# S4 convolution and PEER experts on one core: remainders loaded once, two steps ordered later, more output buffers

## The chip, the cores and the metric

The kernel runs on 1 core of one Trainium2 chip. The metric is device time in microseconds (us), the median of the runs of a kernel. Before the change it is 1446.17 us, of 3 runs (1444.73, 1446.17, 1447.50). The core's engines are TensorE (PE, matmuls), VectorE (DVE), ScalarE (ACT), GpSimd (POOL) and SyncE (SP, which issues the DMAs).

## The reference

The input x is 2048 tokens of 576 channels. Branch `a` is an S4 convolution of the whole sequence; branch `b` is a mixture of 4096 one-neuron experts that are picked by product keys (32 heads, 64 keys per half, the best 2). A gate mixes the two for each token.

```python
def _A_ref(u, ...):
    P = exp(logdA[:, :, None] * l)                      # l = 0..2047
    K = einsum("dn,dnl,dn->dl", Cc, P, dB).real         # kernel, 576 x 2048
    y = irfft(rfft(pad(u)) * rfft(pad(K)))[:L]          # along the sequence
    return y + u * Dskip

def _B_ref(x, w_q, k1, k2, u, v):
    q = einsum("nd,dhc->nhc", x, w_q)                   # 32 heads x 256
    s1, s2 = q[..., :128] @ k1.T, q[..., 128:] @ k2.T   # 64 scores each
    ...                                                 # best 2 of each, best 2 of the 4 sums
    g = softmax(top_s)
    act = gelu(einsum("nd,nhkd->nhk", x, u[top_e]))
    return einsum("nhk,nhk,nhkd->nd", g, act, v[top_e])

g = sigmoid((x * gate_w).sum(-1))
return g * _A_ref(x, ...) + (1 - g) * _B_ref(x, ...)
```

## The kernel before

Nothing is gathered. The kernel computes all products of tokens and experts (`a` matmuls, x by u) and all scores (`s` matmuls, x by folded queries and keys), and then multiplies by weights that are zero where an expert wasn't picked. Every f32 operand is split in two f16 parts, high and low (`xb`, `uhl`, `whl`, `vhl`, `wh`), and a product is three matmuls: high by high, high by low, low by high. The channels are 576 = 4 x 128 + 64; the 64 left over are the remainder (`xr`, `ur`, `wrem`).

**The start.** `x_load` and `u_load` fetch the first 512 tokens of x and the first 512 experts of u: the remainder twice, into both halves of the partitions, and the four blocks of 128 channels in two DMAs (`halves_load`). `scale_first` squares them on ACT as they land (`sq`, into column sums `sc`), and PE adds the sums over the partitions; from that come the scales of the split. Between the two scales `x_norm(0)` runs eight filler matmuls on PE, whose result is overwritten.

**The main part.** `s` and `a` matmuls alternate by 512 columns. Beside them run, as generators: the splits of the next blocks of x, u and the queries; the generation of the convolution kernel K (`kb`); the first stage of a transform in two stages, for u (`u_stage1`: u is scaled and split into `uh`, the `u` matmuls follow, the result goes to `su_d` in DRAM) and for K (`k_stage1`: `k` matmuls into `k1o`, stored to `sk_d`); the products of both and the way back (`products`, with its `back`: `pv` matmuls into `vo`, stored to `z_d`); the selection of experts; and the scaled results of `a`, stored to `g_d`.

**The output stage.** For each of 16 token tiles PE builds the weights from one-hot codes (`S` matmuls of `A` and `Bg`, both made on DVE), DVE multiplies them with the results that were stored (`gl<-S,gl`), ACT and DVE split these (`wh`), and `o` matmuls multiply them by the experts' values. The values are scaled and split by `v_work` in eight chunks of 512 experts (`vhl`): the raw values of chunk c are loaded into the place of chunk c+1, the last into a place of its own (`vs`); the high part is made on ACT, the low part on DVE. `v_work` begins when `v_norm` has all squares of the values. `y` matmuls are the last stage of the transform (`y_part`); `ya` rows are the output.

**What sets the order.** The code is executed once, at build time, by a planner: generators wait in a heap, a clock runs on with every matmul, and an estimate of each engine's time says when a tile is ready. `ready(x, late=...)` holds a generator back until the planner takes x to be ready, plus `late` us. Each engine then runs its instructions strictly in the order in which the planner issued them, with semaphores for the true dependences; all loads and nearly all stores are on one queue, SP's. An edit of a `late` or of a number of buffers therefore moves everything that the planner decides later.

All instructions but a few are recorded in three helpers: L134 (an operation of ACT, DVE or POOL), L205 (a DMA), L214 (a matmul).

Of the kernel before, what the change touches and what calls it, by code (L numbers as in the profile page):

```python
# [24 lines left out]
D = 576  # L25
# [113 lines left out]
def body(ctx: ExitStack, tc: tile.TileContext, xT, au, par, logdt, dskip, gatew, wq, kT, uT, vv,  # L139
# [281 lines left out]
    idx = wj.tile([128, NT, 64, 2], F16, name="idx")  # L421
    xb = []

    def halves_load(a, src, c):

        columns.add(a.tensor.name)
        for m in (0, 2):
            dma(a[:, m:m + 2], src[128 * m:128 * m + 256, c].rearrange("(k p) n -> p k n", p=128))

    def x_load(tb):  # L430
        a = slot([4, 512], F32, f"xs{tb}")
        r = pl.tile([128, 512], F32, tag="xr", name=f"xr{tb}", bufs=2)
        c = slice(512 * tb, 512 * tb + 512)
        if tb > 0:
            dma(a, xT[0:512, c].rearrange("(k p) n -> p k n", p=128))
        dma(r[0:64], xT[512:576, c])
        dma(r[64:128], xT[512:576, c])
        if tb == 0:
            halves_load(a, xT, c)
        return a, r  # L440

    def squares(a, r, sq, dst):

        acc = newcol(), newcol()
        S.activation(sq[:, 0:4, :], a, AF.Square, accum_out=sc[:, acc[0]])
        S.activation(sq[:, 4, :], r, AF.Square, accum_out=sc[:, acc[1]])
        yield from ready(sq)
        tag = side()
        yield from need(tag)
        p = bank(tag, "sq")  # L450
        mm(p[:, 0:2], onesb, short(acc[0].start, 2), True, True, 0.05)
        yield from ready(p)
        V.tensor_reduce(out=dst, in_=p[:, 0:2], axis=AX, op=OP.add)
        free(tag, dst)
# [5 lines left out]
    def x_norm(tb, sq):  # L460

        yield from need("kb")
        p = bank("kb", f"x{tb}")
        if tb == 0:
            for k in range(8):
                mm(p, onesb, sq[:, k % 4, :], True, True)
            while not marks["s"]:
                yield 0.1
        for k in range(5):
            mm(p, onesb, sq[:, k, :], k == 0, k == 4)  # L470
        normed.append(tb)
# [27 lines left out]

    def scale_first(a, r, sq, keep=None):  # L500

        acc = [newcol() for _ in range(3)]
        yield from ready(r)
        S.activation(sq[:, 4], r, AF.Square, accum_out=sc[:, acc[0]])
        for n, m in enumerate((0, 2)):
            yield from ready(a[:, m:m + 2])
            S.activation(sq[:, m:m + 2], a[:, m:m + 2], AF.Square, accum_out=sc[:, acc[n + 1]])
        yield from ready(sq)
        yield from need("kb")
        p = bank("kb", "sq")  # L510
        for n in range(3):
            mm(p[:, 0:1], onesb, short(acc[n].start, 1), n == 0, n == 2, 0.05)
        yield from ready(p)
        out = root_scale(p[:, 0:1], 1.02)
        if keep is not None:
            V.tensor_copy(keep, p[:, 0:1])
        free("kb", out[0])
        return out
# [548 lines left out]
    def u_stage1():  # L1067
# [32 lines left out]
        for p in range(NT):  # L1100
# [7 lines left out]
            V.scalar_tensor_tensor(h[:, 1], a, s_u, h[:, 0], op0=OP.mult, op1=OP.subtract)  # L1108
            if p + 1 < NT:
                load(p + 1)  # L1110
            yield from ready(h)
            while ended[0] < p:
                yield 0.3
            tag = side()
# [23 lines left out]
    def k_stage1(ksb, fk, tabs):  # L1138
# [11 lines left out]
        for w in range(32):  # L1150
            tkt = tabs[w // 16]
            yield from ready(tkt, ksb)
            yield from enter()
            o = fk.tile([128, D], F32, tag="s1o", name=f"k1o{w}", bufs=4)
            pbs = []
            yield from need("wb", 2)
            for hh in range(2):
                pb = bank("wb", f"k1_{w}_{hh}")
                for n in range(2):
                    mm(pb[:, :288], tkt[:, w % 16, n], ksb[:, 2 * hh:2 * hh + 2, :, w, :].rearrange("p j c i -> p (j c) i"),  # L1160
                       n == 0, n == 1)
                pbs.append(pb)
            spawn(tail(w, o, pbs))
            del pb, pbs
# [3 lines left out]
    def products(ff):  # L1168
# [51 lines left out]
        def back(g, v):  # L1220
            for k, c, o, w in pieces(g):
                if k not in vos:
                    vos[k] = ff.tile([128, 2, D], F32, tag="vo", name=f"vo{k}", bufs=2)
            pvs = [bank("wb", f"pv_{g}_{n}") for n in range(2)]
            for n, (rows, cols) in enumerate(quads):
                mm(pvs[n // 2][cols, 0:PW], fi[rows, cols], v[rows, n % 2, :], True, True, 0.11)
            spawn(store(g, pvs))
# [85 lines left out]
    def u_load(c):  # L1313
# [6 lines left out]
        dma(r[64:128], uT[512:576, cs])  # L1320
        if c == 0:
            halves_load(a, uT, cs)
        return a, r

# [2 lines left out]
    def u_build(c):  # L1327
# [12 lines left out]
        if c == 0:  # L1340
            first_u[0] = hl
            s, i = yield from scale_first(a, r, sq, nu[:, 0:1])
            marks["s"].append(1)
        else:
            yield from squares(a, r, sq, nu[:, c:c + 1])
            s, i = root_scale(nu[:, c:c + 1], 1.02)
        if len(xb) == 4:
            V.tensor_scalar(i_a[:, c, :], i_x, i, None, op0=OP.mult)
# [510 lines left out]
```

## Time and profile before

| what | us |
|---|---|
| median of 3 runs | 1446.17 |
| the profiled execution, its time | 1444.99 |
| its span in the trace | 1443.2 |
| PE busy | 1422.5 |
| DVE busy | 1160.0 |
| ACT busy | 769.7 |
| POOL busy | 484.7 |
| first matmul of `a` starts at | 15.91 |
| first matmul of `S` starts at | 953.50 |
| first matmul of `o` starts at | 994.3 |

The span is 1.8 us shorter than the time of the same execution: what lies around it isn't in the trace. Times within the trace count from the start of the span. A row of the timeline reads: start, length, engine, line, operation, out<-in, shape, count; in brackets the time for which the engine stood idle before it, and what ended that. A row with a count of several is a run of such instructions, and its length reaches to the end of the last. Matmuls overlap, so the start of the next row says more than the length of one.

### The profile page before, as it was taken

How to read it: one execution, taken by the hardware profiler on the slowest of the kernel's cores; microseconds unless marked ns; L12 is line 12 of the kernel's file. 1: busy time of each engine (PE TensorE's matmuls, PEld its weight loads, DVE VectorE, ACT ScalarE, POOL GpSimd, SP SyncE). 2: the span in 40 equal slices, each digit the busy share in tenths (PEclk: the TensorE clock that was granted, in tenths of full speed). 3: DMA queues.
4: the chain of work that ended last, by engine and by line, in shares of the span. 5: the costliest groups of instructions: out<-in, count | busy, mean ns of one | idle time of the engine just before them, and what ended most of it. 6: DMA issues, size and time to landing. Idle time of an engine off the chain costs nothing.

```text
span 1443.2 us, 40781 instructions
## 1 busy us (share of the span) xinstructions
PE 1422.5 (99%) x16153; PEld 836.1 (58%) x16153; DVE 1160.0 (80%) x4590; ACT 769.7 (53%) x1277; POOL 484.7 (34%) x492
## 2 busy tenths in 40 slices
PE   7999999999999999999999999999999999999999
PEld 3444545455455445455555444456787787787785
DVE  6899899879886997875899897689877777867840
ACT  6346876786784876744655555666333224323310
POOL 0325347557266346230447899701000000000000
PEclk9999999999999999999999999999999999999999
DMA  9234323342334323159675677878433332442400
GB/s 309 74 114 154 105 74 120 124 145 72 108 100 154 93 87 120 49 173 310 210 259 196 241 257 275 274 234 262 156 124 127 126 122 86 142 149 69 159 10 18
DMA packets 134369, 215.70 MB, mean 149 GB/s; under 512 B 11041, under 2 KB 79905, under 8 KB 127777
## 3 DMA queue, kind: packets, MB, share of 16 engines
q1 hardware_dynamic: 134080, 213.06, 45.1%
q8 instruction: 127, 2.08, 0.6%
q14 instruction: 66, 0.53, 0.1%
q10 hardware_dynamic: 96, 0.02, 0.0%
HBM read 141.74 MB, written 71.30 MB: 148 GB/s over the span
## 4 chain that ended last, share of the span: by engine, by line
PE 86%; DVE 5%; DMA 1%; issue 0%; ACT 0%; SPq 0%; DVEq 0%; ACTq 0%
PE o L214 25%; PE s L214 24%; PE a L214 22%; PE S L214 3%; PE kb L214 2%; PE wb L214 2%; PE pr L214 2%; PE y L214 1%; PE kP L214 1%; PE pv L214 1%; PE u L214 1%; DVE vhl L134 1%; PE k L214 1%; DMA z_d<-vo 1%; DVE gl L134 1%; DVE A L134 1%
## 5 line engine op out<-in xcount | busy, mean ns | idle before, releaser
L214 PE MATMUL o<-vhl,wh 128*128 128x288 f16 (+2 forms) x3072 | 382.8, 286 | 0.0
L214 PE MATMUL s<-whl,xb 128*128 128x512 f16 x1536 | 363.9, 379 | 0.0
L214 PE MATMUL a<-xb,uhl 128*128 128x512 f16 x1536 | 358.9, 379 | 0.2 <-DVE go L134 0.2
L214 PEld LDWEIGHTS <-wh 128*128 128x128 f16 x3072 | 292.4, 98 | 84.1 <-issue 3.7
L214 PEld LDWEIGHTS <-xb 128*128 128x128 f16 x1792 | 170.7, 98 | 209.8 <-issue 15.2
L214 PEld LDWEIGHTS <-uhl 128*128 128x128 f16 x1536 | 147.7, 98 | 177.0 <-issue 3.5
L134 DVE FIND_INDEX8 i<-m,s 128x8 uint32<-128x64 f32 x1024 | 206.1, 219 | 0.0
L134 ACT ACTIVATE wh<-gl,s_wg 128x1024 f16<-128x1024 f32 x64 | 69.0, 1137 | 197.2 <-DVE gl L134 197.2
L134 DVE MAX8 m<-s 128x8 f32<-128x64 f32 x1024 | 145.8, 212 | 28.7 <-PE s L214 28.0
L134 POOL TENSOR_TENSOR CS<-CS,ex 128x512 f32<-128x512 f32 x72 | 98.0, 1392 | 147.5 <-DVE ex L134 146.1
L134 DVE TENSOR_TENSOR gl<-S,gl 128x256 f32<-128x256 f32 x256 | 88.4, 413 | 36.8 <-PE S L214 36.8
L134 ACT ACTIVATE go<-a,i_a 128x512 f32<-128x512 f32 x93 | 62.6, 685 | 94.5 <-PE a L214 68.4
L134 POOL TENSOR_TENSOR e<-aN,rt 128x512 f32<-128x512 f32 x72 | 83.3, 1178 | 49.9 <-PE kb L214 43.7
L134 DVE TENSOR_TENSOR A<-iota_a,vals 128x2048 f16<-128x2048 f16 x64 | 77.9, 1218 | 23.3 <-PE S L214 23.3
L134 ACT ACTIVATE gl<-gl 128x1024 f32<-128x1024 f32 x64 | 63.6, 1045 | 45.3 <-DMA gl<-g_d 45.3
L134 DVE SCALAR_TENSOR_TENSOR wh<-gl,s_wg,wh 128x1024 f16<-128x1024 f32 x62 | 77.6, 1279 | 12.4 <-ACT wh L134 12.3
L214 PE MATMUL s<-wrem,xb 128*128 128x512 f16 x256 | 76.2, 379 | 0.0
L214 PE MATMUL a<-xb,wrem 128*128 128x512 f16 x256 | 75.9, 379 | 0.0
L134 DVE MATCH_VALUE_LOAD i<-m,s 128x8 f32 x1024 | 69.4, 68 | 0.1
L134 ACT ACTIVATE CS<-CS 128x1024 f32<-128x1024 f32 x57 | 59.2, 1044 | 7.5 <-DVE CS L134 7.5
L134 POOL TENSOR_TENSOR ex<-ex,gN 128x512 f32<-128x512 f32 x36 | 44.8, 1255 | 53.2 <-ACT ex L134 53.0
L134 DVE SCALAR_TENSOR_TENSOR ya<-o,om,ya 128x288 f32<-128x288 f32 (+2 forms) x32 | 15.2, 513 | 54.9 <-PE o L214 54.9
(205 smaller groups left out, 2098.7 us busy)
## 6 DMA issues: line engine op xcount, KB each, us to landing
g_d<-go SPq DMA_DIRECT2D x128, 256.0 KB, 2.5
gl<-g_d SPq DMA_DIRECT2D x32, 1024.0 KB, 5.5
wq<-in_wq_dram SPq DMA_DIRECT2D x16, 1152.0 KB, 5.7
su_d<-us SPq DMA_DIRECT2D x32, 288.0 KB, 2.6
sk_d<-k1o SPq DMA_DIRECT2D x32, 288.0 KB, 2.9
ui<-su_d SPq DMA_DIRECT2D x16, 576.0 KB, 3.9
ki<-sk_d SPq DMA_DIRECT2D x16, 576.0 KB, 5.5
vn<-in_vv_dram SPq DMA_DIRECT2D x32, 288.0 KB, 5.4
```

The lines of the kernel that those rows point to most:

```text
L134: return f(*a, **k)
L214: T.matmul(o, l, r, start=start, stop=stop)
```

## The change

1. The first remainders of x and u are loaded once, into partitions 0 to 63; DVE copies them to 64 to 127. ACT squares 64 rows of them instead of 128, and memsets clear what isn't written. The four blocks of 128 channels come in three DMAs (two blocks, one, one) and are squared in three pieces, so four column sums are added on PE instead of three, for x and for u. Six fillers are left of eight.
2. The matmul on the squares of the second block of experts waits for the planner's estimate plus 2.0 us.
3. The `u` matmuls of the first two position transforms wait for the estimate of `uh` plus 1.8 us.
4. `k1o` has six buffers instead of four, `vo` three instead of two.

```diff
+    PARTS = ((0, 2), (2, 1), (3, 1))
     def halves_load(a, src, c):
         columns.add(a.tensor.name)
-        for m in (0, 2):
-            dma(a[:, m:m + 2], src[128 * m:128 * m + 256, c].rearrange("(k p) n -> p k n", p=128))
+        for m, n in PARTS:
+            dma(a[:, m:m + n], src[128 * m:128 * m + 128 * n, c].rearrange("(k p) n -> p k n", p=128))
...
         dma(r[0:64], xT[512:576, c])
-        dma(r[64:128], xT[512:576, c])
-        if tb == 0:
+        if tb > 0:
+            dma(r[64:128], xT[512:576, c])
+        else:
             halves_load(a, xT, c)
...
-    def squares(a, r, sq, dst):
+    def squares(a, r, sq, dst, late=0.0):
...
-        yield from ready(sq)
+        yield from ready(sq, late=late)
...
         if tb == 0:
-            for k in range(8):
+            for k in range(6):
                 mm(p, onesb, sq[:, k % 4, :], True, True)
...
     def scale_first(a, r, sq, keep=None):
-        acc = [newcol() for _ in range(3)]
+        acc = [newcol() for _ in range(1 + len(PARTS))]
+        if keep is None:
+            V.memset(sq[64:128, 4], 0.0)
+        V.memset(sc[64:128, acc[0]], 0.0)
         yield from ready(r)
-        S.activation(sq[:, 4], r, AF.Square, accum_out=sc[:, acc[0]])
-        for n, m in enumerate((0, 2)):
-            yield from ready(a[:, m:m + 2])
-            S.activation(sq[:, m:m + 2], a[:, m:m + 2], AF.Square, accum_out=sc[:, acc[n + 1]])
+        S.activation(sq[0:64, 4], r[0:64], AF.Square, accum_out=sc[0:64, acc[0]])
+        V.tensor_copy(r[64:128], r[0:64])
+        for n, (m, w) in enumerate(PARTS):
+            yield from ready(a[:, m:m + w])
+            S.activation(sq[:, m:m + w], a[:, m:m + w], AF.Square, accum_out=sc[:, acc[n + 1]])
...
-        for n in range(3):
-            mm(p[:, 0:1], onesb, short(acc[n].start, 1), n == 0, n == 2, 0.05)
+        for n, c in enumerate(acc):
+            mm(p[:, 0:1], onesb, short(c.start, 1), n == 0, n == len(PARTS), 0.05)
...
-            yield from ready(h)
+            yield from ready(h, late=1.8 if p < 2 else 0.0)
...
-            o = fk.tile([128, D], F32, tag="s1o", name=f"k1o{w}", bufs=4)
+            o = fk.tile([128, D], F32, tag="s1o", name=f"k1o{w}", bufs=6)
...
-                    vos[k] = ff.tile([128, 2, D], F32, tag="vo", name=f"vo{k}", bufs=2)
+                    vos[k] = ff.tile([128, 2, D], F32, tag="vo", name=f"vo{k}", bufs=3)
...
-            yield from squares(a, r, sq, nu[:, c:c + 1])
+            yield from squares(a, r, sq, nu[:, c:c + 1], 2.0 if c == 1 else 0.0)
```

(`u_load` changes as `x_load` does.) Three places of the order follow. On PE, where the square-sum of the second block of experts stands (`s_8` is the ninth group of scores; a row without "x" is one instruction), the order before has it behind three matmuls of that group:

```order
L214 MATMUL s_8_920<-whl_152,xb_519 128x512
L214 LDWEIGHTS xb_519
L214 MATMUL s_8_920<-whl_152,xb_519 128x512
L214 LDWEIGHTS xb_519
L214 MATMUL s_8_920<-whl_152,xb_519 128x512
L214 LDWEIGHTS onesb
L214 MATMUL sq<-sc,onesb 128x2
L214 LDWEIGHTS xb_519
L214 MATMUL s_8_920<-whl_152,xb_519 128x512
```

and the order of the change has it behind twelve, ahead of the two matmuls on the remainder:

```order
L214 MATMUL s_8_927<-whl_156,xb_526 128x512
L214 LDWEIGHTS xb_526
L214 MATMUL s_8_927<-whl_156,xb_526 128x512
L214 LDWEIGHTS onesb
L214 MATMUL sq<-sc,onesb 128x2
L214 LDWEIGHTS xb_526
L214 MATMUL s_8_927<-wrem_116,xb_526 128x512
L214 LDWEIGHTS xb_526
L214 MATMUL s_8_927<-wrem_116,xb_526 128x512
```

So it moved behind nine more matmuls. On PE again, where the second position transform (`u_1`) begins, before:

```order
L214 MATMUL s_14_1260<-whl_152,xb_598 128x512
L214 LDWEIGHTS xb_598
L214 MATMUL s_14_1260<-whl_152,xb_598 128x512
L214 LDWEIGHTS tu_1032
L214 MATMUL u_1_0_0_1286<-uh_1210,tu_1032 128x288
```

and with the change:

```order
L214 MATMUL s_14_1267<-wrem_116,xb_605 128x512
L214 LDWEIGHTS xb_605
L214 MATMUL s_14_1267<-wrem_116,xb_605 128x512
L214 LDWEIGHTS xb_605
L214 MATMUL s_15_1300<-whl_156,xb_605 128x512
L214 LDWEIGHTS xb_605
L214 MATMUL s_15_1300<-whl_156,xb_605 128x512
L214 LDWEIGHTS xb_605
L214 MATMUL s_15_1300<-whl_156,xb_605 128x512
L214 LDWEIGHTS tu_1006
L214 MATMUL u_1_0_0_1320<-uh_1217,tu_1006 128x288
```

Before it stood behind the ninth matmul of `s_14`; now it stands eight matmuls later, behind the third of `s_15`. The third place is on DVE, at the beginning of the output stage, where the last chunk of values (`vhl<-vs`) is split. Before, the first pair stands right ahead of these rows, and the second ends them, among the one-hot codes (`A`, `Be`, `Bg`) of the third tile, and its first `gl`:

```order
L134 TENSOR_TENSOR iwv<-sci 128x1
L134 TENSOR_SCALAR om<-gA 128x16
L134 TENSOR_SCALAR om<-om,iwv 128x16
L134 SCALAR_TENSOR_TENSOR wh_1_13596<-gl_0_13137,s_wg,wh_0_13595 128x1024
L134 TENSOR_TENSOR A_3_13854<-iota_a,vals 128x2048
L134 TENSOR_TENSOR Be_3_13856<-iota_b,vals 128x512
L134 TENSOR_TENSOR Bg_3_13858<-Be_3_13856,vals 128x512 x2
L134 TENSOR_TENSOR gl_0_13609<-S_0_0_13722,gl_0_13609 128x16x16
L134 TENSOR_TENSOR gl_1_13610<-S_0_0_13722,gl_1_13610 128x16x16
L134 TENSOR_TENSOR gl_0_13609<-S_0_1_13723,gl_0_13609 128x16x16
L134 TENSOR_TENSOR gl_1_13610<-S_0_1_13723,gl_1_13610 128x16x16
L134 SCALAR_TENSOR_TENSOR vhl_12500<-vs,sci,vhl_12500 128x576 x2
```

With the change they stand behind all sixteen `gl` of the third tile, among the rows of `ya` and two `wh`:

```order
L134 TENSOR_TENSOR ya_13645<-ya_13645,db 128x576
L134 TENSOR_TENSOR ya_13646<-ya_13646,db 128x576
L134 SCALAR_TENSOR_TENSOR vhl_12542<-vhl_12543,sci,vhl_12542 128x576 x2
L134 SCALAR_TENSOR_TENSOR ya_13645<-y_0_0_14120,iuk,ya_13645 128x288
L134 SCALAR_TENSOR_TENSOR ya_13645<-y_0_1_14125,iuk,ya_13645 128x288
L134 SCALAR_TENSOR_TENSOR wh_1_14088<-gl_0_13594,s_wg,wh_0_14087 128x1024
L134 SCALAR_TENSOR_TENSOR vhl_12543<-vs,sci,vhl_12543 128x576 x2
L134 SCALAR_TENSOR_TENSOR ya_13646<-y_1_0_14130,iuk,ya_13646 128x288
L134 SCALAR_TENSOR_TENSOR ya_13646<-y_1_1_14135,iuk,ya_13646 128x288
L134 SCALAR_TENSOR_TENSOR wh_1_14088<-gl_0_13594,s_wg,wh_0_14087 128x1024
L134 SCALAR_TENSOR_TENSOR vhl_12543<-vs,sci,vhl_12543 128x576 x2
```

What moved: from the `A` row that waits for the first `S` matmul to the last of these pairs, DVE has 9 sets of `A`, `Be` and two `Bg` in both orders; 36 `gl` before and 48 now; 10 pairs of `vhl` and 13; 5 `wh` and 9; and the six rows of `ya`, which stood behind. On PE, between the first `S` matmul and the second half of the eighth chunk of the first tile's `o`, there are 768 `S`, 180 `o` and 16 `y` in both, and 156 `a` before and 137 now. POOL makes one of the `wh` there instead of two.

More of the change, by code (lines that the diff above doesn't have):

```diff
@@ L1319, in u_load @@
         dma(r[0:64], uT[512:576, cs])
-        dma(r[64:128], uT[512:576, cs])
-        if c == 0:
+        if c:
+            dma(r[64:128], uT[512:576, cs])
+        else:
             halves_load(a, uT, cs)
```

## The prediction

> **What bounds the kernel now.** I read the page first, then the waits of TensorE (PE), then the timeline at each place that the change touches.
>
> ```profile
> span 1443.2 us, 40781 instructions
> PE 1422.5 (99%) x16153; PEld 836.1 (58%) x16153; DVE 1160.0 (80%) x4590; ACT 769.7 (53%) x1277; POOL 484.7 (34%) x492
> PEclk9999999999999999999999999999999999999999
> PE 86%; DVE 5%; DMA 1%; issue 0%; ACT 0%; SPq 0%; DVEq 0%; ACTq 0%
> ```
>
> PE is busy for 99% of the span at the full granted clock, and it is 86% of the chain that ended last. The change does not lessen its matmuls in any amount that counts: per source one more tiny square-sum and, once, two fewer fillers. So the time can move only where PE waits. The view of waits lists them, as engine, what waited, what it waited for, total us, times, longest:
>
> ```profile
> PE sq L214 <- ACT xb L134: 10.0, 3, 5.1
> PE sq L214 <- ACT uhl L134: 1.6, 1, 1.6
> PE k L214 <- ACT k1o L134: 1.4, 1, 1.4
> PE kb L214 <- issue: 1.4, 1, 1.4
> PE u L214 <- DVE uh L134: 1.4, 1, 1.4
> PE S L214 <- DVE gl L134: 0.7, 2, 0.5
> PE pv L214 <- ACT vo L134: 0.7, 1, 0.7
> ```
>
> Each edit has a row here: the remainders the first, the later squares the second, the later low words the fifth, six k1o buffers the third, three vo buffers the seventh. All but the first add up to 5.1 us. That is the size of the game: a third of a percent.
>
> **The change part by part.**
>
> *Remainders loaded once, blocks in three pieces.* The start, ScalarE (ACT) first:
>
> ```profile
> 4.35 0.63 ACT L134 ACTIVATE xb<-xr 128x512 bf16<-128x512 f32 x1 [2.12 <-DMA xr<-in_xT_dram]
> ...
> 6.96 1.06 ACT L134 ACTIVATE xb<-xs 128x1024 bf16<-128x1024 f32 x1 [1.89 <-DMA xs<-in_xT_dram]
> ...
> 9.09 1.06 ACT L134 ACTIVATE xb<-xs 128x1024 bf16<-128x1024 f32 x1 [0.98 <-DMA xs<-in_xT_dram]
> ...
> 11.21 1.06 ACT L134 ACTIVATE uhl<-us 128x1024 bf16<-128x1024 f32 x1 [0.36 <-DMA us<-in_uT_dram]
> ...
> 12.60 1.06 ACT L134 ACTIVATE uhl<-us 128x1024 bf16<-128x1024 f32 x1 [0.24 <-DMA us<-in_uT_dram]
> ```
>
> ```profile
> 10.31 3.57 PE L214 MATMUL x<-xb,onesb 128*128 128x512 bf16 x8
> 13.68 0.28 PE L214 MATMUL sq<-sc,onesb 128*128 128x1 bf16 x3
> 13.82 2.30 PE L214 MATMUL x<-xb,onesb 128*128 128x512 bf16 x5
> 15.91 0.52 PE L214 MATMUL a<-xb,uhl 128*128 128x512 f16 x1
> ```
>
> The squares follow the landings. Two halves of x, 512 KB each, landed 2.13 us apart (6.96, 9.09), so the 128 KB saved per source are worth 0.53 us: u's first half lands 0.5 to 1.1 us earlier, near 10.5. Behind it ACT needs 1.06 + 0.63 + 0.63 and the readout, and would be done near 13.0 instead of 13.7. I take 0.7 us (0.3 to 1.1; the number of transfers stays 8, so their issue costs nothing more). VectorE (DVE) copies the missing 64 rows while it waits for the first square-sum: nothing.
>
> The eight fillers run from 10.31 to 13.68, at 0.42 us each, up to u's square-sum without a hole. Six of them, from about 9.6, would end near 12.1, some 0.9 us ahead of that sum: a new hole in PE, a rival below.
>
> The Trainium skill, "TensorE: Matmul & The Clock Gate", under "What's actually happening", says that PE runs at half rate until a window of about 3.4 us was busy. The trace agrees with the slow start (0.42 us per 512 columns there, 0.22 later), though its clock row shows 9 from the first slice. By that rule a window that holds the hole would not count as busy, and the sum would be up to 1.7 us more (1451.3, an estimate from the rows above and this page); by the rows alone, where work broken by waits ran before 10.31 too, it stays as it is.
>
> *Squares and low words later.* One 512-column matmul takes 0.22 us (eight of s in 1.73 us):
>
> ```profile
> 79.71 1.89 PE L214 MATMUL s<-whl,xb 128*128 128x512 f16 x8
> 81.44 0.59 PE L214 MATMUL s<-wrem,xb 128*128 128x512 f16 x2
> ```
>
> The square-sum of the second expert block now stands nine matmuls later, 1.9 us, more than the 1.6 us that PE waited: gain 1.6 (bounds 0 and 1.6). The u matmuls of the second position transform stand eight later, 1.7 us. But their operand comes from DVE:
>
> ```profile
> 117.26 1.41 DVE L134 SCALAR_TENSOR_TENSOR uh<-us,sci,uh 128x576 f16<-128x576 f32 x1
> ...
> 60.00:126.00 66.00, 62.99 (x338) 28.88 (x337) 65.25 (x383) 24.98 (x46) 27.75 (x22) 1.00 0.34 105
> ```
>
> In this stretch (columns: length, then PE, PEld, DVE, ACT, POOL busy) DVE is busy for 65.25 of 66.0 us, so its uh moves only with the start. PE comes 1.6 earlier for the vanished hole and 1.7 later for the move: about 1.2 of the 1.4 us stay. Gain 0.2 (bounds 0 and 1.4).
>
> *Buffers.* k matmuls wait 1.4 us once for a k1o buffer whose store is late; two more buffers cover two more pairs of 0.4 us work and the s matmuls between them: gain 1.4 (bounds 0 and 1.4). The third vo buffer takes 0.7 (bounds 0 and 0.7). What is late next in both cases is PE itself.
>
> Gains: 0.7 + 1.6 + 0.2 + 1.4 + 0.7 = 4.6 us.
>
> *What the new order brings.* The planner replays everything after the two moved steps differently. Between 126 and 690 us PE was busy for 562.4 of 564, so a new wait there would cost as the rows above do, 1.4 to 1.6 us each; I take none (bounds 0 and 3, below nothing 1.4 if the kb row goes).
>
> One place can be worked out: where experts' values are split for the output stage. The first S matmuls release DVE here:
>
> ```profile
> 954.51 1.23 DVE L134 TENSOR_TENSOR A<-iota_a,vals 128x2048 f16<-128x2048 f16 x1 [1.32 <-PE S L214]
> ...
> 956.78 1.41 DVE L134 TENSOR_TENSOR gl<-S,gl 128x256 f32<-128x256 f32 x4
> 958.11 1.53 DVE L134 SCALAR_TENSOR_TENSOR vhl<-vhl,sci,vhl 128x576 f16<-128x576 f32 x2
> 959.56 1.41 DVE L134 TENSOR_TENSOR gl<-S,gl 128x256 f32<-128x256 f32 x4
> ...
> 963.43 2.74 DVE L134 TENSOR_TENSOR gl<-S,gl 128x256 f32<-128x256 f32 x8 [1.00 <-PE S L214]
> ...
> 968.20 1.27 DVE L134 SCALAR_TENSOR_TENSOR wh<-gl,s_wg,wh 128x1024 f16<-128x1024 f32 x1
> 969.40 1.54 DVE L134 SCALAR_TENSOR_TENSOR vhl<-vhl,sci,vhl 128x576 f16<-128x576 f32 x2
> ...
> 974.25 2.35 DVE L134 TENSOR_TENSOR Be<-iota_b,vals 128x512 f16<-128x512 f16 x1
> ...
> 1003.36 3.42 DVE L134 SCALAR_TENSOR_TENSOR vhl<-vs,sci,vhl 128x576 f16<-128x576 f32 x2
> ...
> 1011.90 1.54 DVE L134 SCALAR_TENSOR_TENSOR vhl<-vs,sci,vhl 128x576 f16<-128x576 f32 x2
> ```
>
> From the starts: a set A, Be, Bg takes 2.27 us, four gl 1.33, a pair of vhl 1.45, a wh 1.20. From the row at 954.51 to the last vhl pair the order before has 9 sets, 36 gl, 10 pairs, 5 wh and 1.0 us of small rows: 20.4 + 12.0 + 14.5 + 6.0 + 1.0 = 53.9 us. Measured are 58.9 (to 1013.4). The 5.0 between are the wait of 1.0 at 963.43 and two rows that were 1.9 longer than their like, at 974.25 and 1003.36; the second lies beside this one on GpSimd (POOL):
>
> ```profile
> 1002.89 2.54 POOL L134 TENSOR_TENSOR wh<-gl,wh 128x1024 f16<-128x1024 f32 x1 [26.56 <-ACT gl L134]
> 1017.21 1.42 DVE L134 TENSOR_TENSOR ya<-ya,db 128x576 f32<-128x576 f32 x2
> 1022.10 0.94 DVE L134 SCALAR_TENSOR_TENSOR ya<-y,iuk,ya 128x288 f32<-128x288 f32 x2
> 1019.53 6.67 PE L214 MATMUL o<-vhl,wh 128*128 128x288 f16 x53
> ```
>
> In the order of the change the same stretch has 9 sets, 48 gl, 13 pairs, 9 wh and the six ya: 20.4 + 16.0 + 18.9 + 10.8 + 3.2 + 0.3 = 69.6 us, 15.7 more. POOL has one such wh left instead of two: 1.9 less. So the last pair is done 13.8 us later after the first S than before.
>
> PE needs this pair in the second half of chunk 7 of the first o tile. Before, that is the 31st o matmul after 1019.53, at 0.126 us each: 1023.3, and the pair was done at 1013.4, 9.9 us of slack. In the new order PE has 19 fewer matmuls of a between the first S and that place (137 for 156): it comes 4.1 us sooner. 13.8 + 4.1 - 9.9 = **8.0 us of new wait**. Behind the waiting matmul the whole o stage is queued on PE, and nothing in it can be caught up. If the 1.0 and the last 1.9 also went, it would be 5.1; if both POOL rows' worth stayed, 9.9. I take 8.0, since the 53.9 and its three extras explain before to 0.1 us.
>
> Sum: 1444.99 (the profiled execution) - 4.6 + 8.0 = 1448.4. The median of the runs shown, 1446.17, is 1.2 above that execution, so **1449.6 us** on its scale.
>
> **The rivals.**
>
> *The extras fall away* (not slower). POOL's subtraction may lengthen nothing if it falls beside other DVE rows, and PE may not keep DVE waiting at the third S group. The wait is then 5.1, and 1446.17 - 4.6 + 5.1 = 1446.7. For it: POOL's row moves. Against: both rows beside POOL were lengthened before. It decides below 7.5 us of wait (4.6 + 2.9), from where the change is not slower by 0.2%.
>
> *The splits are not late* (faster): the buffers and moves do what they say, and DVE reaches the last pair before PE. 1446.17 - 4.6 = 1441.6. Against it stand the 15.7 us of added DVE rows in a stretch where DVE was already busy for 74.0 of 76 us:
>
> ```profile
> 954.00:1030.00 76.00, 75.27 (x1166) 48.44 (x1159) 74.02 (x131) 41.94 (x52) 4.77 (x2) 1.00 0.67 215
> ```
>
> *The hole behind six fillers keeps PE slow.* If PE stays at 0.42 us per matmul for another eight or so, it loses up to 1.7 us: 1451.3. For it: the first a matmul at full rate came only after 5.6 us of unbroken work. Against: the hole is under 1 us, and the work after it is unbroken. This is the rule of the page named above, as a case of its own.
>
> *A new wait in the reshuffled part*, two of 1.5: 1452.6. Nothing in the profile names its place.
>
> **How the numbers follow.** Forecast 0.42, extras gone 0.26, not late 0.20, slow PE 0.05, new waits 0.07. A measurement of this kernel can tell about 0.2%, 2.9 us: slower begins at 1449.1, faster ends at 1443.3. The forecast lies on that line, so I give it 0.30 slower and 0.12 within; with the two last rivals slower is 0.42. Within: 0.12 + 0.26 = 0.38. Faster 0.20. The range has to reach into the faster case and up to a wait of 9.9 with one new wait (1446.17 - 4.6 + 9.9 + 1.5 = 1453.0): 1442 to 1453. The slower half's own range is 1447.5 to 1453.
>
> **What would show it.** The row of sq on uhl gone; u on uh still near 1.2; k on k1o and pv on vo gone. The first a near 15.2 instead of 15.91, with a hole ahead of u's square-sum. Above all a new row, o waiting for DVE vhl, of some 8 us in all at chunks 5 to 7 of the first tile. If that row is under 2 us the forecast is wrong, and the time is near 1441.6; if PE shows waits of over 2 us between 126 and 900, my zero there is wrong.

## The result, and the profile after

| | before | with the change |
|---|---|---|
| median (us) | 1447.04 (6 runs, 1444.73 to 1448.15) | 1455.18 (6 runs, 1453.76 to 1457.61) |
| ratio, 95% interval | 1 | 1.0062 [1.0052, 1.0073] |
| span of the profiled execution (us) | 1443.2 | 1452.0 |

The change makes the kernel slower by 0.6%, 8 to 9 us. The page's first lines, answering to those of before (its clock row shows no dip, since one figure stands for 36 us):

```profile
span 1452.0 us, 40768 instructions
...
PE 1425.5 (98%) x16151; PEld 836.3 (58%) x16153; DVE 1166.4 (80%) x4606; ACT 769.5 (53%) x1276; POOL 470.7 (32%) x487
...
PEclk9999999999999999999999999999999999999999
...
PE 83%; DVE 7%; DMA 1%; ACT 1%; issue 1%; SPq 0%; DVEq 0%; ACTq 0%
```

PE is busy 3.0 us longer with two matmuls fewer in the records, so some of its work ran slower; and it waits more. The waits of PE, as engine, what waited, for what, us in total, times, longest:

```profile
PE sq L214 <- ACT xb L134: 8.1, 4, 4.6
PE wn L214 <- ACT wj L134: 4.5, 2, 3.3
PE o L214 <- DVE vhl L134: 4.3, 3, 1.9
PE S L214 <- DVE gl L134: 1.5, 2, 1.0
PE pv L214 <- DVE i L134: 1.1, 1, 1.1
PE o L214 <- issue: 0.8, 1, 0.8
PE u L214 <- DVE uh L134: 0.7, 1, 0.7
```

The waits that the edits aimed at are gone or shorter: sq on uhl of the second block, k on k1o and pv on vo are gone; u on uh is 0.7 for 1.4; the start waits 8.1 for 10.0, and 0.6 more on u's squares. Two new ones of over 4 us stand above the rest. The second is the one that the prediction worked out. The first, at 645 us, is the wait of `wn`, the square-sum of a half of the queries' weights (`wq`), for the squares of it on ACT (`wj`). PE there, in the timeline:

```profile
641.82 2.75 PE L214 MATMUL s<-whl,xb 128*128 128x512 f16 x12
644.40 0.59 PE L214 MATMUL s<-wrem,xb 128*128 128x512 f16 x2
648.34 0.16 PE L214 MATMUL wn<-sc,onesb 128*128 128x1 bf16 x1 [3.34 <-ACT wj L134]
649.62 0.16 PE L214 MATMUL wn<-sc,onesb 128*128 128x1 bf16 x1 [1.12 <-ACT wj L134]
```

and around both places the work of the engines in windows (length, busy PE, PEld, DVE, ACT, POOL, then granted clock, DMA share, GB/s):

```profile
612.00:645.00 33.00, 33.00 (x169) 14.96 (x170) 32.81 (x242) 19.69 (x30) 2.10 (x2) 1.00 0.22 75
645.00:650.00 5.00, 0.54 (x4) 0.28 (x4) 4.90 (x28) 4.54 (x10) 0.00 (x0) 0.98 0.16 61
650.00:654.00 4.00, 4.00 (x13) 1.51 (x12) 3.90 (x21) 0.00 (x0) 0.00 (x0) 0.60 0.00 0
1014.00:1018.00 4.00, 3.97 (x77) 2.76 (x78) 4.00 (x8) 0.75 (x2) 0.00 (x0) 0.63 0.60 174
1026.00:1031.00 5.00, 1.63 (x12) 1.17 (x12) 5.00 (x7) 4.16 (x5) 0.00 (x0) 1.00 0.75 232
```

The clock is the second thing to see: behind the wait at 645 it is 0.60 for four us, and behind the S waits at 1012 0.63. There 14 matmuls took 4.7 us (649.65 to 654.35) for 3.0, and 24 o matmuls 4.7 us for 3.0. Each of the two places so shows 1.7 us of slower work beside its waits. Whether that adds to the loss is a question of its own, answered for the o tile below.

For the experiments I compare traces by PE's lag: the time at which PE has done the same amount of work as in the trace of before (each kind of matmul counted at the median distance of its starts there), less the time before. The columns are microseconds of such work and not of time: 130 is reached at 148 us of the trace before, 600 at 645, 620 at 665, 660 at 707, 900 at 973 and 951 at 1024. Single executions differ by up to 2 us at the start, and where orders differ the measure itself is good to 1 us or so; the steps between columns say more than the columns. The changed kernel, in us:

| work done | 130 | 600 | 620 | 660 | 900 | 951 | end |
|---|---|---|---|---|---|---|---|
| changed kernel | -4.0 | -6.6 | +0.9 | -0.2 | +1.3 | +8.5 | +9.6 |

(The end is 0.8 above the difference of the spans, the two fillers that the change hasn't.) The gains are larger than forecast, 6.6 us by 600 here and 4.8 to 6.5 in the nine other traces of this order and start below. 7.5 go at the `wn` place and 7.2 in the first o tile.

### The profile page after: what moved, and what is told of

Its sections match the earlier page's. It is cut to its first block, busy times and chain, and to the rows that moved or that the text cites. A ratio compares the mean times of both kernels' runs of the same rounds, so it can differ in the third digit from the quotient of the medians.

```text
span 1452.0 us, 40768 instructions
## 1 busy us (share of the span) xinstructions
PE 1425.5 (98%) x16151; PEld 836.3 (58%) x16153; DVE 1166.4 (80%) x4606; ACT 769.5 (53%) x1276; POOL 470.7 (32%) x487
## 4 chain that ended last, share of the span: by engine, by line
PE 83%; DVE 7%; DMA 1%; ACT 1%; issue 1%; SPq 0%; DVEq 0%; ACTq 0%
PE o L214 25%; PE a L214 22%; PE s L214 21%; PE S L214 3%; PE kb L214 2%; PE pr L214 2%; PE wb L214 2%; PE kP L214 1%; DVE i L134 1%; PE k L214 1%; PE pv L214 1%; PE y L214 1%; DVE gl L134 1%; PE u L214 1%; DVE m L134 1%; DVE vhl L134 1%
## 5 line engine op out<-in xcount | busy, mean ns | idle before, releaser
L214 PE MATMUL o<-vhl,wh 128*128 128x288 f16 (+2 forms) x3072 | 385.1, 287 | 5.1 <-DVE vhl L134 4.3
L214 PE MATMUL s<-whl,xb 128*128 128x512 f16 x1536 | 365.0, 381 | 0.0
L214 PE MATMUL a<-xb,uhl 128*128 128x512 f16 x1536 | 359.5, 379 | 0.5 <-ACT uhl L134 0.3
L214 PEld LDWEIGHTS <-wh 128*128 128x128 f16 x3072 | 293.1, 98 | 91.0 <-issue 9.6
L214 PEld LDWEIGHTS <-xb 128*128 128x128 f16 x1792 | 170.8, 98 | 210.0 <-issue 16.0
L214 PEld LDWEIGHTS <-uhl 128*128 128x128 f16 x1536 | 146.9, 98 | 176.5 <-issue 3.7
L134 DVE FIND_INDEX8 i<-m,s 128x8 uint32<-128x64 f32 x1024 | 206.0, 219 | 0.0
L134 DVE MAX8 m<-s 128x8 f32<-128x64 f32 x1024 | 145.7, 211 | 28.7 <-PE s L214 28.3
L134 ACT ACTIVATE wh<-gl,s_wg 128x1024 f16<-128x1024 f32 x64 | 69.1, 1137 | 185.4 <-DVE gl L134 185.4
L134 POOL TENSOR_TENSOR CS<-CS,ex 128x512 f32<-128x512 f32 x72 | 94.5, 1346 | 144.9 <-DVE ex L134 144.9
L134 DVE TENSOR_TENSOR gl<-S,gl 128x256 f32<-128x256 f32 x256 | 88.2, 413 | 38.1 <-PE S L214 38.1
L134 ACT ACTIVATE go<-a,i_a 128x512 f32<-128x512 f32 x82 | 55.5, 683 | 93.3 <-PE a L214 62.0
L134 POOL TENSOR_TENSOR e<-aN,rt 128x512 f32<-128x512 f32 x72 | 82.9, 1172 | 49.7 <-PE kb L214 44.3
L134 DVE TENSOR_TENSOR A<-iota_a,vals 128x2048 f16<-128x2048 f16 x64 | 77.9, 1217 | 20.6 <-PE S L214 20.6
L134 DVE SCALAR_TENSOR_TENSOR wh<-gl,s_wg,wh 128x1024 f16<-128x1024 f32 x63 | 78.8, 1278 | 12.3 <-ACT wh L134 12.3
L134 ACT ACTIVATE gl<-gl 128x1024 f32<-128x1024 f32 x64 | 63.6, 1045 | 45.5 <-DMA gl<-g_d 39.7
L214 PE MATMUL s<-wrem,xb 128*128 128x512 f16 x256 | 76.2, 379 | 0.0
L214 PE MATMUL a<-xb,wrem 128*128 128x512 f16 x256 | 75.9, 379 | 0.0
L134 ACT ACTIVATE CS<-CS 128x1024 f32<-128x1024 f32 x62 | 64.3, 1044 | 19.5 <-DVE CS L134 19.5
L134 POOL TENSOR_TENSOR ex<-ex,gN 128x512 f32<-128x512 f32 x36 | 45.2, 1266 | 89.7 <-ACT ex L134 89.7
L134 DVE MATCH_VALUE_LOAD i<-m,s 128x8 f32 x1024 | 69.0, 67 | 0.1
L134 DVE SCALAR_TENSOR_TENSOR ya<-o,om,ya 128x288 f32<-128x288 f32 (+2 forms) x32 | 15.2, 513 | 56.7 <-PE o L214 56.7
```

What stands on the lines that cost most here:

```text
L134: return f(*a, **k)
L214: T.matmul(o, l, r, start=start, stop=stop)
```

## The experiments

All ratios are to before, timed on the same chip. First the change was taken apart. The start and the buffers leave the order behind them as it was; the two late steps alone bring the new order.

**Start and buffers, without the late steps.**

```diff
-            yield from squares(a, r, sq, nu[:, c:c + 1], 2.0 if c == 1 else 0.0)
+            yield from squares(a, r, sq, nu[:, c:c + 1])
...
-            yield from ready(h, late=1.8 if p < 2 else 0.0)
+            yield from ready(h)
```

> Before, with the first remainders loaded once, six fillers, six k1o and three vo buffers, but without the two late steps; the order on every engine behind the start is that of before. Theory 1 (only the re-planning behind the late steps costs): first a near 13.8 us instead of 15.9 (gain 2.1), no wait of k on k1o (1.4) and of pv on vo (0.7): 4.2 us faster, near 0.997 of before. Rival (the smaller start or the buffers cost by contention for SBUF or the DMA queue): gain under 2 us, with new waits on PE in an unchanged order.

Measured: ratio 0.9976 [0.9966, 0.9986], 1442.95 us for 1445.88. First a at 14.26; no wait on k1o or vo is left, and PE's lag stays flat behind the k stage (-2.6 at 660, -3.3 at 900 and 951, -2.7 at the end). Theory 1 holds, at 2.9 us of the 4.2 expected (3.5 by the ratio): the first a came 0.5 later than expected, and u on uh waited 2.0 for 1.4, since PE came to it sooner.

**The late steps alone.**

```diff
-            yield from squares(a, r, sq, nu[:, c:c + 1])
+            yield from squares(a, r, sq, nu[:, c:c + 1], 2.0 if c == 1 else 0.0)
...
-            yield from ready(h)
+            yield from ready(h, late=1.8 if p < 2 else 0.0)
```

> Before with the two late steps alone. The order behind them is that of the change, on every engine. Theory 1: the loss of the change without the 4.2 us of start and buffers, so 8.1 + 4.2 = 12 us slower than before, ratio near 1.0085; waits of PE on wn (4.5) and in the first o tile (4.3), as in the changed kernel. Rival: 4 to 6 us slower, the rest of the change's loss being due to start and buffers.

Measured: 1.0127 [1.0112, 1.0142], 18.2 us slower. The whole loss is theirs, and more than expected: `wn` waits twice here, at 647 and at 771 us (8.8 us in all); in the changed kernel the second wait isn't there. The waits of o on vhl are like those of the changed kernel (5.0 for 4.3).

**The later square-sum alone, and the later low words alone.**

> Before with the later square-sum of the second expert block alone; this gives a third order. Worked out from its rows, DVE has the last pair of values some 40 us ahead of PE, so no wait in the first o tile. Theory 1 (what the late steps cost is the order that the planner happens to draw): the wait of sq on uhl (1.6) goes, and waits elsewhere are those of a new order, 0 to 6 us: from 1.6 faster to 4.5 slower. Rival (a later square-sum itself delays the chain of the expert blocks): waits of a on uhl, in each later block.

> Before with the later low words of the first two position transforms alone; a fourth order. From its rows the last pair of values comes to DVE 16.5 us after PE wants it (9.1 by the same count in the changed kernel, -8.9 before). Theory 1: PE waits some 14 to 16 us in the first o tile, 12 to 18 us slower, ratio 1.008 to 1.012. Rival (the count is not what sets this wait): o waits under 5 us.

Measured: 1.0066 [1.0053, 1.0078] and 1.0098 [1.0083, 1.0113]. The first gives no wait on values, as counted, and no wait of a on the blocks' splits above 0.3; it loses in many small ones elsewhere (u on uh 3.2, wn on wj 2.4, o on issue 2.2, a 1.8 and k 1.6): 8.4 us slower, where I allowed 4.5. The second has the o tile late as counted: between the first S matmul and the o matmul that needs the last low row, PE took 14.7 us more than its work there (expected 14 to 16). Its waits there, in the view of 990 to 1040 us, are of many kinds:

```profile
PE o L214 <- DVE vhl L134: 2.8, 3, 1.8
PE S L214 <- DVE Bg L134: 2.5, 1, 2.5
PE S L214 <- DVE gl L134: 1.9, 2, 1.4
PE y L214 <- DVE gl L134: 0.6, 1, 0.6
PE y L214 <- DMA yz<-z_d: 0.6, 1, 0.6
PE S L214 <- DVE ya L134: 0.3, 1, 0.3
```

and the same stretch in a window:

```profile
990.00:1040.00 50.00, 40.97 (x744) 29.63 (x744) 49.80 (x90) 28.14 (x35) 2.76 (x1) 0.90 0.64 211
```

DVE is busy for 49.8 of 50 us, so where PE stops, or runs at a lower clock (0.90 over the window), is only where it happens to need a row of DVE; the sum is set by DVE's rows. The rival read one row ("o waits under 5 us" is true) and missed the sum.

**The first o tile.** The low rows of the values' last three chunks are left out on DVE (POOL writes zeros in their place).

```diff
+                        low = V.scalar_tensor_tensor
+                        if c >= 5:
+                            V.account("scalar_tensor_tensor", h[:, j, 1, :], x, sv[0], h[:, j, 0, :], op0=OP.mult, op1=OP.subtract)
+                            low = lambda o, *a, **k: nc.gpsimd.memset(o, 0.0)
-                        V.scalar_tensor_tensor(h[:, j, 1, :], x, sv[0], h[:, j, 0, :], op0=OP.mult, op1=OP.subtract)
+                        low(h[:, j, 1, :], x, sv[0], h[:, j, 0, :], op0=OP.mult, op1=OP.subtract)
```

(`account` runs the planner's clock on without an instruction, so that the order stays. The added lines move the helpers: L141 and L221 below are L134 and L214.)

> The changed kernel, with the same order, but the low halves of the values' chunks 5 to 7 are zeros written by POOL, and the 12 rows of DVE for them are left out (8.7 us of DVE work ahead of the first o tile's last chunk). Theory 1 (DVE is late there, and that costs waits and then a lower clock): the waits of o on vhl (4.3 us) go, the waits of S on gl fall from 1.5 to under 0.5, and the stretch behind them keeps the full clock: 7 us less than the changed kernel, ratio to before 1.0062 - 0.0048 = 1.0014. Rival (the lower clock there has another cause): 4.3 us less, ratio 1.0032.

Measured: 1.0031 [1.0019, 1.0043], 4.5 us less than the changed kernel by the ratios. In the trace the place itself falls from 7.2 us of lag to 0.5: no wait of o on vhl is left, and the clock stays full behind the S waits.

```profile
PE S L221 <- DVE gl L141: 1.2, 2, 0.8
PE o L221 <- issue: 0.9, 1, 0.9
```

```profile
1014.00:1030.00 16.00, 14.77 (x247) 10.92 (x246) 13.93 (x30) 6.64 (x10) 1.88 (x4) 1.00 0.79 253
```

(the first from the view of waits, the second a window behind the S matmuls). Of Theory 1 the waits hold, but the total is the rival's number: this execution lost 4.5 us in the stage of products (660 to 900), the changed kernel's 1.5. The S waits fell only to 1.2. The full clock was partly luck: in two later kernels without these rows (exp and sine rows left out too; index rows as well) it fell behind the same S waits, and the tile cost 2.2 and 2.0.

With the low rows in place the lower clock adds nothing to the tile's loss. The tile costs 7.2 to 7.3 us of lag in all six traces of this order that have them. In four the clock fell behind the S waits; in two (the late steps alone, and the exp and sine rows left out) it stayed at 1.00, and there PE waited longer instead, 5.0 for o on vhl and 0.4 to 0.5 for y on gl. DVE's rows set the end of the tile either way.

**The place at 645 us, one thing at a time.** First PE's wait alone was taken away: the `wn` of that half sums the columns of the half before.

```diff
+    last_acc = [None]
...
-            mm(p[:, 0:1], onesb, short(acc[n].start, 1), n == 0, n == 1, 0.03)
+            mm(p[:, 0:1], onesb, short((last_acc[0] if (c, h) == (5, 0) else acc)[n].start, 1), n == 0, n == 1, 0.03)
+        last_acc[0] = acc
```

> The changed kernel, with the same order, but the wn matmuls of the eleventh half of the queries' weights sum the columns of the half before, so that they don't wait for the squares of their own half on ACT; ACT's work stays. Theory 1 (PE loses 4.5 us waiting there and 1.9 at the lower clock behind it): 6.4 us less than the changed kernel, ratio 1.0062 - 0.0044 = 1.0018. Rival (DVE is behind at that time, and PE would be stopped by the scores' banks a little later): under 3 us less, with a new wait of s or a on DVE between 645 and 690.

> Both edits of the two runs before in one kernel. Theory 1 (two separate places make up the loss): 13.4 us less than the changed kernel, ratio 0.9970, near that of before with start and buffers alone. Rival (something else in the new order costs too): above 0.999.

Measured: 1.0068 [1.0055, 1.0081] and, with the low rows left out too, 1.0022 [1.0013, 1.0032]. Nothing was gained at 645 us: PE ran on to the next thing that was late (all its waits between 630 and 670 us):

```profile
PE u L214 <- DVE uh L134: 3.9, 1, 3.9
```

That was the rival's case, though on u and not on s or a; with the low rows left out too the ratio is the rival's as well (above 0.999). Next, DVE's share: half of its index rows in the fifth block of scores were left out.

```diff
+            if c == 4 and g >= 4:
+                V.account("max_index", out=i8[:, q, g, :], in_max=m8[:, q, g, :], in_values=pb[:, 64 * g:64 * g + 64])
+                if g == 4:
+                    nc.gpsimd.memset(i8[:, q, 4:8, :], 0)
+                continue
             V.max_index(out=i8[:, q, g, :], in_max=m8[:, q, g, :], in_values=pb[:, 64 * g:64 * g + 64])
```

> The changed kernel, with the same order, but for the fifth block of scores (16 groups, 609 to 667 us) half of the FIND_INDEX8 rows of DVE and their match loads are left out (4 of 8 per group, about 1.0 us each group); POOL writes zeros in their place. Theory 1 (DVE is what is late there: eleven groups of scores in a row with no a between, each 3.3 us on DVE and 3.0 on PE, with splits on top): the waits of wn on wj (4.5) go, no wait of u on uh takes their place, and the clock stays full: 6.4 us less than the changed kernel, ratio 1.0018. Rival (ACT is late by its own queue, two table loads and the exp and sine rows ahead of the squares): over 2 us of wait stay, ratio above 1.004.

> The run before, and the low halves of the values' chunks 5 to 7 left out on DVE as in the run on these alone. Theory 1: both places where DVE is late are gone, 13 us less than the changed kernel, ratio 0.997. Rival (the stage of products, which stood 2 to 4 us later in all runs with this order, is a third place that costs): ratio 0.999 to 1.001.

Measured: 1.0075 [1.0062, 1.0089] and 1.0038 [1.0024, 1.0052]. My theory fell, and the first rival, ACT's own queue, held: DVE had 6 us of idle time there now, and `wn` on `wj` was as in the changed kernel (4.5, 2, 3.3). The second ratio lies above its rival's range too. The changed kernel's ACT says why, in its timeline:

```profile
635.06 0.78 ACT L134 ACTIVATE us<-u 128x288 f32<-128x288 f32 x2 [1.88 <-PE u L214]
635.86 1.28 ACT L134 ACT_TABLE_LOAD   x1
...
640.21 1.28 ACT L134 ACT_TABLE_LOAD   x1
...
644.55 1.04 ACT L134 ACTIVATE CS<-CS 128x1024 f32<-128x1024 f32 x1
...
647.04 1.15 ACT L134 ACTIVATE wj<-wq 128x1152 bf16<-128x1152 f32 x1
...
649.39 0.19 ACT L134 ACTIVATION_READ_ACCUMULATOR wj<-wq 128x1 f32 x1
```

From the copy of PE's u to the end of the squares ACT has 14.5 us of rows without a hole, in their order: two table loads, the exponentials and sines of the last step of K, some small rows, and only then the squares. PE had 9.7 us of scores (635.3 to 645.0) between its u and `wn`. So ACT's eight exp and sine rows, and with them both table loads, were left out (`account` for K's step 35), first alone, then with the low rows:

```diff
+            act = (lambda *a, **k: S.account("activation", *a, **k)) if c == 35 else S.activation
-            S.activation(e, e, AF.Exp)
-            S.activation(ex, ex, AF.Exp)
+            act(e, e, AF.Exp)
+            act(ex, ex, AF.Exp)
...
-            S.activation(v[:, 0:2], v[:, 0:2], AF.Sin, scale=-TWO_PI, bias=halfpi)
-            S.activation(v[:, 2:4], v[:, 2:4], AF.Sin, scale=-TWO_PI)
+            act(v[:, 0:2], v[:, 0:2], AF.Sin, scale=-TWO_PI, bias=halfpi)
+            act(v[:, 2:4], v[:, 2:4], AF.Sin, scale=-TWO_PI)
```

> The changed kernel, with the same order, but the eight exp and sine rows of K's last step on ACT are left out, with their two table loads (9.6 us of ACT's queue between the copy of u at 635 us and the squares at 647 us). Theory 1 (ACT's queue is what is late): the waits of wn on wj fall from 4.5 to about 2 us, where the load of the weights takes over, no wait of u on uh follows, and the clock behind stays full: 3 to 5 us less than the changed kernel, ratio 1.003 to 1.004. Rival (the load decides already): waits of over 4 us stay, ratio above 1.005.

> The run before, and the low halves of the values' chunks 5 to 7 left out on DVE. Theory 1: the two places add up, 8 to 11 us less than the changed kernel, ratio 0.9985 to 1.0007. Rival (gains in one are lost in the products' stage, which differs from run to run with this order): above 1.002.

Measured: 1.0054 [1.0042, 1.0066] and 1.0009 [0.9998, 1.0020], both a little above what theory 1 gave; the first lies in the range of the rival, whose sign, waits of over 4 us on `wn`, is not there. ACT's queue did hold `wn`, and behind it DVE held u (the waits of PE between 630 and 670 us):

```profile
PE u L221 <- DVE uh L141: 2.4, 1, 2.4
PE wn L221 <- ACT wj L141: 1.1, 1, 1.1
```

The place cost some 6.6 us of lag still. With both cuts, DVE's and ACT's:

> The changed kernel, with the same order, with both cuts of the place near 645 us: half of DVE's index rows of the fifth block of scores, and ACT's exp and sine rows of K's last step. Theory 1 (two engines are late there at once, because PE has 150 matmuls of s and none of a ahead of wn): waits of wn on wj near 1 us, none of u on uh; the place costs 1 to 2 us instead of 7, so some 5.5 us less than the changed kernel, ratio 1.0022. Rival (a third thing, such as the load of the queries' weights or of the next block): waits of over 3 us in that place, ratio above 1.004.

> The run before, and the low halves of the values' chunks 5 to 7 left out on DVE. Theory 1: with both places out, what is left is the gain of start, late steps and buffers, less 1 to 3 us in the products' stage: ratio 0.9965 to 0.9985, near that of before with start and buffers (0.9976). Rival (a third place of the new order takes the rest): ratio above 1.000.

Measured: 1.0035 [1.0021, 1.0048] and 0.9985 [0.9976, 0.9994], the first between the two theories by the ratio, the second at the upper end of what theory 1 gave. Between 630 and 670 us one wait is left:

```profile
PE wn L221 <- ACT wj L141: 0.9, 1, 0.9
```

Now the place costs 2.2 us instead of 7.5, and with the low rows left out as well the kernel is 11.1 us faster than the changed one, faster than before. PE's lag in these traces:

| work done | 600 | 620 | 660 | 900 | 951 |
|---|---|---|---|---|---|
| changed kernel | -6.6 | +0.9 | -0.2 | +1.3 | +8.5 |
| index rows halved | -5.8 | +1.8 | +1.0 | +3.7 | +10.9 |
| exp and sine rows left out | -5.8 | +0.9 | +0.5 | +2.8 | +10.0 |
| both | -5.1 | -2.9 | -3.3 | -1.4 | +5.8 |
| both, and low rows left out | -5.0 | -2.9 | -3.0 | +0.2 | +2.2 |
| start and buffers (order of before) | -1.3 | -1.3 | -2.6 | -3.3 | -3.3 |

Read along the rows: 600 to 620 is the `wn` place, 900 to 951 the o tile. Between 660 and 900, the stage of products, the kernels of the new order lose 1.5 to 3.2 us in this table (4.5 in the trace with the low rows alone, 4.9 with low and index rows), and that of the old order gains 0.7. The three traces that lose over 3 us there have a wait of the products' matmuls (`pr`) for the load of `ui`, 1.7 to 1.9, where the others have 0.2 at most. This third place was not taken apart; it stays open.

**A shorter late step.** The planner draws the old order as long as the square-sum is held back by 1.4 us or less; from 1.6 on it draws another. So 1.0 was tried, on top of start and buffers:

```diff
+            yield from squares(a, r, sq, nu[:, c:c + 1], 1.0 if c == 1 else 0.0)
-            yield from squares(a, r, sq, nu[:, c:c + 1])
```

> Before with start and buffers, and the square-sum of the second expert block held back by 1.0 us instead of 2.0. On PE it stands seven matmuls later; nothing else moves on any engine. Theory 1 (the later place itself is good, the re-planning is what cost): the wait of sq on uhl, 1.0 us in the run with start and buffers, goes: ratio 0.9970 to 0.9975. Rival (a later square-sum delays the splits of that block): no gain over start and buffers alone, and waits of a on uhl.

Measured: 0.9976 [0.9966, 0.9985], the same as without it. The wait of sq on uhl went (1.0 us), and u on uh took it:

```profile
PE u L214 <- DVE uh L134: 2.8, 2, 1.4
```

for 2.0 without the step. The ratios can't tell the theories apart, since half a microsecond is less than the interval; the waits can. The later place does no harm, as no a waits on uhl, and 0.8 of the 1.0 us that it gains is lost again at u on uh: DVE, busy for 65.2 of the 66 us from 60 to 126, sets that wait.

**The fillers.** On the order of before with start and buffers, without fillers and with eight:

```diff
-            for k in range(6):
-                mm(p, onesb, sq[:, k % 4, :], True, True)
+            clock[0] += 6 * (512 / 2400 + 0.003)
```

```diff
             for k in range(6):
                 mm(p, onesb, sq[:, k % 4, :], True, True)
+            for k in range(2):
+                mm(p, onesb, sq[:, k % 4, :], True, True, 0.0)
```

> Before with start and buffers (ratio 0.9976 so far), same order, but without any filler. Theory 1 (the fillers bring PE to its full rate before the first a matmuls): the first five x and some fourteen a matmuls take 0.43 us instead of 0.22, some 3 us lost less what waits anyway: ratio 0.9986 to 0.9996. Rival (the waits at the start hide it): no difference.

> Before with start and buffers, same order, but with eight fillers as before. Theory 1 (the hole of about 1 us behind six fillers costs nothing, since the full rate was reached behind it): no difference to six, ratio 0.9976. Rival (the hole sometimes keeps PE at half rate, as in one profile of the short late step, where five x matmuls took 2.3 us): up to 1.5 us less, ratio 0.9966.

Measured: 1.0006 [0.9997, 1.0015] without, 0.9983 [0.9974, 0.9992] with eight, 0.9976 with six. So six and eight are the same within their intervals, and none costs 0.3%, 4 us, more than theory 1 gave. The first matmuls behind, without fillers and with six (start and buffers):

```profile
12.60 2.29 PE L214 MATMUL x<-xb,onesb 128*128 128x512 bf16 x5
14.69 3.61 PE L214 MATMUL a<-xb,uhl 128*128 128x512 f16 x12
```

```profile
12.67 1.24 PE L214 MATMUL x<-xb,onesb 128*128 128x512 bf16 x5
14.26 2.76 PE L214 MATMUL a<-xb,uhl 128*128 128x512 f16 x12 [0.35 <-ACT uhl L134]
```

From there on PE is 1.2 us behind, at the thirteenth a as at the three-hundredth. The two spans differ by 3.1 us; the rest comes later, in part as a wait of k for the load of `ksb` (1.1), and no run shows that it follows from the fillers.

## Why the prediction was right and wrong

**Right: the sign, and the o tile.** The prediction gave slower as the likeliest, for the reason that is in the trace. Its count of DVE's rows, 69.6 us with 1.0 and 1.9 of extras, makes 72.5 from the `A` row that the first S matmuls release to the end of the last low rows. The changed kernel has 72.7, from the first of these rows to the end of the second:

```profile
959.11 1.23 DVE L134 TENSOR_TENSOR A<-iota_a,vals 128x2048 f16<-128x2048 f16 x1 [1.62 <-PE S L214]
...
1030.32 1.53 DVE L134 SCALAR_TENSOR_TENSOR vhl<-vs,sci,vhl 128x576 f16<-128x576 f32 x2
```

The wait of 8.0 came out as 7.2 of lag. Its form was not as told: 4.3 us of o on vhl, 0.8 more of S on gl, and 1.7 at a lower clock, for which other traces of this order show longer waits. The same count gave 14 to 16 us for another order, where 14.7 were measured. The row of 8 us in all that was to show it has 4.3.

**Wrong: the bounds of the term for the reshuffled part.** The step that failed reads "I take none (bounds 0 and 3 ...)"; the sign that the prediction named for it, a wait of over 2 us between 126 and 900, is in the trace (3.34 at 645). The step priced a new wait by the single waits of the old order, 1.4 to 1.6 each, and gave two of them a chance of 0.07. One place there cost 7.5 us: 4.5 of waits, 1.7 of lower clock and some 1 behind it (this last 1 us is in all traces of the order, also where 0.9 of wait is all that is left, and may be an error of the measure). The premise was that a new order would be as good as the old outside the place that I had counted. In the 33 us ahead of this `wn` the old order has 40 a and 98 s matmuls; in the new one PE has 140 s from 612 to 645 us, with 22 u among them and no a. DVE is busy 32.8 of 33.0 us there, with ACT behind PE too. Removing one of the late things only showed the next. With both cuts there the ratio was 1.0035, which is 1451.2 us on the prediction's scale (1446.17 times 1.0035), inside the range. That it then comes near the forecast of 1449.6 is partly luck, since gains that were larger than forecast stand against a loss in the stage of products that was not forecast.

**Wrong in size: the gains.** 4.6 us were forecast, of which 2.5 stand ahead of the two buffer edits, and the lag was -6.6 at 600 us of work. The start gave 2.1 (first a at 13.78 for 15.91; forecast 0.7, at most 1.1), and 1.5 to 1.7 in three other traces (first a at 14.24 to 14.45): the landings came earlier than worked out, with u's square-sum done at 12.2 where 13.0 was forecast, and the first five x matmuls ran at 0.25 us each where they had taken 0.42. The low words gave 0.7 for 0.2. The kb wait of 1.4 is not in the new list, which was allowed for but not taken. The k stage gave 1.9 for 1.4 (lag from 640 to 650 us of work).

**Right: that buffers and start cost nothing, and that the hole does no harm.** k on k1o and pv on vo are gone (pv waits 1.1 for DVE now, a different cause). The rival of the slow PE behind six fillers isn't seen in the medians (0.9976 with six, 0.9983 with eight). Single executions differ: in the trace of the shorter late step, with six, the five x matmuls took 2.3 us, as before; in those of the changed kernel and of start and buffers 1.2.

**Rivals.** "The splits are not late" is refuted by the o row. "The extras fall away" is refuted by the 72.7 us, which would be 69.6 without them, and by the 7.2 of lag; the o row alone, 4.3, would lie nearer to its 5.1 than to 8.0. That the planner's new order costs was one of the rivals, at 0.07 and with two waits of 1.5 us; it is half of the loss.

## What to carry to other kernels

Where a planner sets the order, an edit in one place can be an edit of everything behind it (here 1.4 us in one `late` left the order alone and 1.6 did not): check by the order whether it re-plans, and keep the edits that don't apart from those that do. Here the parts that leave the order alone are worth 0.24% together, and the two that move it cost 1.3%. In a new order, count the in-order rows of each engine between two fixed points against PE's work between them, on ACT as on DVE, at every place where PE meets another engine; one such count was good to 1 us, and the place that wasn't counted cost as much. A wait is no price by itself: behind it may stand the next late engine, or a lower clock; and where another engine's rows set the end of a place, the same loss can show as waits or as slower work.

## What the hardware showed that was not expected

The granted clock falls after short waits. In the changed kernel waits of 1.03 and 0.47 us within the S matmuls of the third tile were followed by 0.63 from 1014 to 1018 us, while 0.26 and 0.47 at the same place before were followed by full clock. The same two waits (1.03 to 1.06, and 0.47) stand in five more traces: in three the 24 o matmuls behind them were slow too (4.2 to 4.7 us for 3.0), in two the clock stayed at 1.00. With the low rows left out the waits are 0.75 to 0.77 and 0.47; the clock stayed at 1.00 behind them in three traces and fell in two. One of these is that with the exp and sine rows left out as well, as its window shows (the clock is the number behind the POOL column):

```profile
1008.00:1020.00 12.00, 10.77 (x187) 8.06 (x186) 11.93 (x26) 4.15 (x7) 4.28 (x8) 0.86 0.85 259
```

Two waits of 1.9 us with twelve o matmuls between them (1026 to 1031) left it at 1.00. The same waits with a different outcome point to where they fall in time; that was not tested.

The Trainium skill, "TensorE: Matmul & The Clock Gate", under "What's actually happening", has the clock fall after a free-running window of some 3.4 us without work. The trace agrees for the waits of 3.34 and 1.12 us, 4.5 in all with one one-column matmul between them (0.60 behind them), and a free-running window would fit the two outcomes above. That 1.5 us of waits within the S matmuls, and even 1.2, can do the same is less than the page has, and the measurement decides.
